# A fused recurrent attention and gated MLP kernel: another order table

## The chip, the cores and the metric

The kernel runs on one core of a Trainium2 chip. The metric is the device time of one execution in microseconds (us); the time of the kernel before is the median of three runs. A core has five engines that matter here, each with its own queue of instructions that it works through in order: TensorE (PE in the profile; PEld are its weight loads), VectorE (DVE), ScalarE (ACT), GpSimd (POOL), and SyncE (SP), which here only issues transfers. Sixteen DMA engines move the data.

## The reference

Four sequences of 768 steps go through a recurrent gated linear attention with 8 heads of width 48; its output, 4 x 768 x 384, is the input of a gated MLP that mixes over positions.

```python
for t in range(S):
    state = alpha[:, :, t, :, None] * state + np.einsum('bhd,bhe->bhde', k[:, :, t], v[:, :, t])
    y[:, :, t] = np.einsum('bhd,bhde->bhe', q[:, :, t], state)
...
h = np.maximum(x @ w_in, 0.0)                      # 384 x 1024
u, v = (h[..., :d_ff // 2].copy(), h[..., d_ff // 2:].copy())
v_n = (v - mu) / np.sqrt(var + 1e-06)
v_s = np.einsum('ts,bsd->btd', w_spatial, v_n) + b_spatial[None, :, None]
return ((u * v_s) @ w_out).astype(np.float32)      # 512 x 384
```

The inputs q, k, v and alpha are 4 x 8 x 768 x 48 in float32, and the result is float32.

## The kernel before

The recurrence is cut into 24 chunks of 128 positions, six for each sequence. Within a chunk the steps become matmuls: cumulated logarithms of alpha, scaled keys and queries, a masked score matrix, and a state that is handed on from chunk to chunk. The first eight chunks are worked in four pairs (numbered 0 to 3, function `pair`), whose loads bring two chunks at once (384 KB); the other sixteen are worked one by one (function `first`, loads of 192 KB). As soon as a sequence's chunks are done, its MLP follows in groups of matmuls (functions `second_v`, `second_u`, `second_s`, `second_o`; all through `group`, whose matmuls are recorded under line 828).

All this is made into 1,141 operations, each a few instructions for one engine. Their names are a kind and numbers, and the text uses them:

- `ac`, `kc`, `qc`, `vc` with a chunk's number (a pair's first chunk): the loads of alpha, k, q, v, all issued on SyncE's queue in the order of the table (lines 441 and 646).
- `ln`, `cum`, `einv`, `eexp`: logarithm (ScalarE), cumulated sum (TensorE, lines 461 and 666), and the exponentials of it with both signs (ScalarE, lines 469, 478, 678, 695). For a pair they are called `lnp`, `cump` and so on, with the pair's number and a half.
- `kt`, `qt` (for a pair `ktp`, `qtp`): the scaled keys (GpSimd, line 690; for a pair GpSimd or VectorE, line 483) and queries (VectorE, lines 490 and 700). `vb`, `vbp`: the values cast to bf16 (GpSimd or ScalarE).
- `trk` (line 719), for a pair `tr_k`, `tr_q` (line 511): their transposes on TensorE; `ev`: the copies of the transposes out of PSUM (VectorE or ScalarE).
- `sc` and `m`: scores (TensorE, lines 583 and 754) and their mask (VectorE, lines 594 and 765). `upd`, `z`, `S`, `sb`: the state's update (TensorE, lines 553 and 740), sum (VectorE), decay (GpSimd, line 344) and bf16 copy (`sbd`, GpSimd or VectorE, line 199).
- `ya`, `y`: the chunk's output (lines 610, 623, 776, 782). `xs`, `xt`, `xe`: its copy, its transposes (lines 374 and 398) and the copies of these.
- `v`, `bn`, `rs`, `vn`: the v half of the first MLP product, its statistics (lines 893, 894) and the normalized rows. `u`: the u half, relu'd by ScalarE or VectorE. `s` and `g`: the spatial mix (a group of six matmuls, often in two parts) and the gating product (GpSimd, line 989). `o`, `st`: the last product and its store (line 1046).
- `cast_w_in`, `cast_w_sp`, `cast_w_out`: casts of the weights out of a float32 buffer `raw_w`. Those of the spatial weights go to one of three buffers `w_row`, which `wt` (transposes on TensorE, line 840) reads; three `w_row` buffers are handed out in the order in which the casts are emitted, so the fourth cast needs the buffer that `wt` of the first has read.

Nothing reorders these operations when the kernel is built. The table `PLAN` (lines 57 to 106), found by a search beforehand, names every operation once, and `replay` emits them in that order. A word is the letter of the engine (P TensorE, D VectorE, A ScalarE, G GpSimd, S SyncE, Q a transfer's own record), the number of the operation, and for some a list of columns after colons. These are filler: before the operation takes its PSUM bank, `bank` (line 187) emits matmuls of junk with so many columns into it, whose result is overwritten. So the table sets three things: the order on each engine's queue; the engine, for the operations that may run on more than one; and the filler. It also sets indirectly who shares what, since the eight PSUM banks, the `w_row` buffers and the other tiles are given out in turn.

TensorE's array can be used whole (128 x 128) or as tiles of 64 rows (or 32, or 64 columns). The `trk`, `xt`, `wt` transposes of lines 719, 398 and 840, the pair's updates and outputs (lines 553 and 610) and the scores (lines 583 and 754) are tiled; all else is not. When a tiled and an untiled instruction follow each other, that is called a change of tiling.

Of the kernel before, what the change touches and what calls it, by code (L numbers as in the profile page):

```python
# [54 lines left out]
LETTERS = {"P": "PE", "D": "DVE", "A": "ACT", "G": "POOL", "S": "SP", "Q": "DMA"}  # L55

PLAN = """
S34 Q35 S36 Q37 G32 G0 Q33 S38 Q39 S94 Q95 S40 Q41 A42 P53:512:512:192 A54 D1 D2 D56 P43 S96 Q97 S98 Q99 S100 Q101
S163 Q164 S4 Q5 S165 Q166 S167 Q168 P59:464 G58 G48 A44 A45 A55 D46 D57 D47 P249:304 P49 P61 A50 P51 D52 D60 A62 A102
A250 P71:304 P74 P113 P103 D72 D73 D76 D75 P63 P77:172 D65 A114 D116 P119:148 A104 A64 A115 A105 A78 G66 G67 G106 D107  # L60
D117 D68 P79 P81 P111 P121 P247 P109 G3 G69 A108 A82 A80 D120 D122 D112 D110 P83 A84 A171 D248 S169 Q170 S9 Q10 S307
Q308 P131 P134 D133 D136 D132 D135 G70 G118 P172:228 P182 P123:240 A183 A8 A173 A124 P137 P138 A139 A174 G7 G6 D125
P85 G126 D128 D185 G127 G129 G175 P88 P142 P140 A86 A184 D176 D186 A143 A89 P188 P190 P180 P144 P178 A141 A191 A145
A181 P146 G11 G12 S309 Q310 S311 Q312 D130 D87 D179 D90 D189 P157 A187 A177 A158 A147 A13 P197 P200 P192 D199 D201
D198 D194 D202 P151:196 P155 A315 A193 A91 P326 P316 A327 P203 P153 P204 G195 G196 G329 A317 A328 A318 P149 A205 A154
D159 D156 D152 D330 G319 P208 P334 A209 P206 D320 P332 P324 P210 P322 D92 D335 D325 D333 D148 A207 P212 A211 A150 P347
P215 P221 A213 A160 A222 A216 S14 Q15 P223 P227 S18 Q19 D93 D323 D161 D348 D349 D214 G16 G17 A224 A228 P225 P229 A226
A21 P232 A234 D231 D230 D233 G20 P235:300 P238 S313 Q314 G331 G321 P344 P336 S367 Q368 S369 Q370 S22 Q23 S371 Q372
A237 A236 D217 D162 D346 A240 D338 A239 A218 D219 D220 A375 A337 P251 P263 P259 P376 A377 A378 G339 P264 D345 D341
D265 P260 D261 P255 P252 A380 A25 A24 D381 D253 P256 D257 G340 G342 G379 S409 Q410 S373 Q374 S446 Q447 S411 Q412 S413  # L70
Q414 S415 Q416 S26 Q27 S480 Q481 S448 Q449 S482 Q483 S450 Q451 S484 Q485 P383 A385 A417 S452 Q453 S577 Q578 S486 Q487
S581 Q582 S579 Q580 S583 Q584 P244 P241 P350 A246 D384 D245 D242 D243 P390 P354 P418 D392 D391 A351 A355 G262 G343
A420 A382 G254 G266 P279 P352 P271 P356 P393 P272 A353 A357 A419 G421 A422 A394 P280 P361 P386 P275 P395 A362 A424
A396 A31 D273 D423 D281 D387 P425 D397 D427 D426 D363 G282 G388 P276 P358 D277 P398 G258 G389 G278 G30 A399 A454 A359
A28 A488 P405 P432 P267 P455 P401 A402 A457 A456 D29 P291 P489 P268 A490 A459 D406 D433 D400 D434 D360 P283 P428 D269
D460 A492 D429 D493 G458 G491 P435 A284 A292 A436 G274 G461 G270 G430 G431 S648 Q649 S617 Q618 S650 Q651 S611 Q612
S652 Q653 S613 Q614 S690 Q691 S615 Q616 S694 Q695 S654 Q655 S692 Q693 P287 P462 P437 P495 P403 D463 D464 D497 D496
A288 A439 A438 P440 A585 A441 A364 D404 P469 P498 P295 P465 P586 P303 D471 D470 D466 D500 D499 A296 A587 A588 A590
A304 P299 G494 G467 G468 G589 G592 D591 D442 P472 A473 P501 P407 P474 A502 A300 P503 P593 P596 A443 A505 A408 D475
D476 P477 A478 D504 D366 D594 D595 D445 D444 D597 D365 P506 P600 P515 D601 D516 A507 A479 A508 D509 D602 A656 A510  # L80
A619 P517 P525 P513 P519 P529 P657 P533 P620 D511 D512 P526 P530 A514 A659 A658 A621 A661 A622 A698 A624 D518 D520
D527 D531 D662 P545 P534 P699 A701 A700 A703 D625 G598 G599 G660 G626 G623 G528 D535 P546 D547 P630 P627 P664 P537
P603 D631 D665 D704 G548 A629 A628 G632 G663 A604 P538 P634 P605 S728 Q729 S762 Q763 S696 Q697 S730 Q731 S732 Q733
S764 Q765 S766 Q767 D539 A607 A666 A606 D635 D636 P541 P667 P542 G702 G532 P706 P671 D668 D543 D673 D672 G669 G536
G670 G544 G633 P608 P637 P521 A707 A736 A708 A638 P737 P713 P639 P522 P549 D714 D715 D641 D523 A770 A609 A705 A738
A739 G740 A640 A741 D742 P771 P550 P642 A772 P709 P744 A774 A643 A746 D710 D551 D775 D745 D644 G524 S858 Q859 S734
Q735 S929 Q930 S860 Q861 G773 G711 G552 G712 G743 G540 P716 P674 A717 A675 P561 P718 P676 P777 P553 A562 A678 A677
D719 D779 D720 D610 P679 P751 A778 A554 A866 A680 A645 A681 P780 D752 P747 D748 D753 D781 D782 P682 P867 P721 P754
A868 A869 A871 A722 A755 S768 Q769 S862 Q863 A723 A776 D683 D872 P573 P688 P684 G749 G750 G870 P756 P874 D646 D757
D875 D685 D758 A689 A574 D724 A876 P686 P783 P569 P881 A784 P785 A570 A787 A687 A725 D882 D786 D883 P759 P557 A760  # L90
P788 P565 P796 P798 P800 S1042 Q1043 S971 Q972 S892 Q893 S864 Q865 S898 Q899 S896 Q897 A979 A558 A789 A566 A937 A900
S894 Q895 S935 Q936 G873 S975 Q976 S931 Q932 S933 Q934 S973 Q974 S977 Q978 S1008 Q1009 S567 Q568 S1046 Q1047 S559 Q560
S1012 Q1013 S1010 Q1011 S1044 Q1045 S1014 Q1015 D727 D647 D761 D726 P794 P806 D790 A791 D799 D797 D795 D792 D793 D801
P901 P980 P802 P938 P877 P807 A902 A903 A907 A905 A981 A939 A940 A982 A944 A984 P810 P803 A942 G904 D878 G941 G879
D808 D906 D804 G805 G880 G809 G983 D985 D943 P822 P884 P811 D812 A885 P823 P908 P886 P945 D824 P814 P911 P815 D912
D909 D816 G813 G817 G913 G825 A910 A887 A888 A947 A946 P889 A1016 A890 P952 P915 P987 D953 D916 D954 P830 P1017 P831
P818 A988 A1019 A1050 A1018 D917 P948 P819 P1051 D949 A1021 A986 A989 D1022 D832 G950 P834 A1052 G951 G1020 P990 P842
P918 A835 A1054 D820 D991 D1055 A843 A919 P838 P1024 P994 P920 D1025 D921 D995 D996 A839 A1023 G914 G833 G1053 G992
S1048 Q1049 S575 Q576 S836 Q837 S844 Q845 S293 Q294 S289 Q290 S571 Q572 S305 Q306 S301 Q302 S555 Q556 A922 A1026 S297
Q298 S285 Q286 S840 Q841 P826 P955 P827 D828 A956 P1057 P957 P1031 D958 P1027 D1028 D1033 D1032 P997 P923 A1058 A1059  # L100
A959 P969 P1060 A1056 A998 P999 D1062 D1001 D1061 D970 G821 G829 G993 G1029 A1000 A924 P960 P846 P1034 A961 A847 G1030
P1063 A1035 A1064 P1002 P963 P1036 P1065 D925 D891 A1003 D962 D1066 P850 P967 A1067 A1037 D1004 A926 D928 P1068 A964
A1038 P1039 D927 D968 A851 A1005 A1069 A1040 D1006 D1041 D1007 D1070 P965 P854 P1076 P1080 P1078 P1074 D966 A1079 A855
A1071 A1081 D1075 D1072 D1073 D1077 P1094 P1082 P1106 P1086 P1083 P1098 P1095 P1090 P1102 P1087 P1107 P1091 P1103
P1110 P1099 P1111 D1096 D1084 G1085 D1088 D1097 D1108 D1092 D1093 G1089 P1113 D1104 G1109 G1105 D1112 D1100 D1101
P1117 P1121 S852 Q853 S563 Q564 S856 Q857 S848 Q849 A1114 S1115 Q1116 A1118 P1133 S1119 Q1120 A1122 P1125 A1134 S1123
Q1124 P1129 S1135 Q1136 A1126 P1137 S1127 Q1128 A1130 A1138 S1131 Q1132 S1139 Q1140
"""


# [1046 lines left out]
```

## Time and profile before

| what | value |
|---|---|
| median of three runs | 144.78 us (144.51 to 145.1) |
| the profiled execution's own time | 144.51 us |
| its span | 142.7 us |
| granted TensorE clock | 1.00 |
| busy: PE / PEld / DVE / ACT / POOL | 134.7 / 84.8 / 118.3 / 109.3 / 83.4 us |
| DMA | 28.64 MB, mean 201 GB/s |
| longest groups on PE | spatial mix 36.8 us, `u` 18.7 us, `o` 18.7 us, `v` 17.1 us |

The span is the time from the first to the last recorded instruction; the execution's own time has some 1.8 us more around it. Busy times of an engine add up its instructions; matmuls overlap, so a busy TensorE isn't one at its peak. The chain of waits goes back from the last instruction, at each step to what released it, and so names who set the end at each moment; its rows give the start, the length and the engine and line, in us. A row of a timeline gives start and length, engine, line, operation, what it writes and reads, and in brackets how long the engine had been idle before and what ended that. A DMA share near or above 1.00 means that the 16 DMA engines had packets under way all the time.

### The profile page before, as it was taken

What the parts mean: (1) busy time and instruction counts of PE and PEld (TensorE: products, weight loads), DVE (VectorE), ACT (ScalarE), POOL (GpSimd) and SP (SyncE); (2) the same over time, 40 slices, a digit from 0 to 9 for tenths busy, and PEclk for the clock granted to TensorE, in tenths of its full rate; (3) what the DMA queues carried; (4) which work ended last, traced back from release to release, by engine and by line L of the source; (5) the groups of instructions that cost most, each with busy time, mean ns of one, the idle gap of its engine ahead of it and who ended that gap; (6) DMA issues with size and microseconds to landing.
All of it is one profiled execution on the core that took longest, in us unless ns stands there. A gap on an engine that the chain in (4) does not pass through costs nothing.

```text
span 142.7 us, 4968 instructions
## 1 busy us (share of the span) xinstructions
PE 134.7 (94%) x1912; PEld 84.8 (59%) x1923; DVE 118.3 (83%) x291; ACT 109.3 (77%) x282; POOL 83.4 (58%) x146
## 2 busy tenths in 40 slices
PE   7999798899999999999999999999999989999990
PEld 3457575566577656675666665656666656566560
DVE  7279878989989699999998898989979779994940
ACT  3477759999888969889987999997978978940061
POOL 6703977366339776982389999410799993000720
PEclk9999999999999999999999999999999999999999
DMA  4999999999998999999999998999998794113045
GB/s 106 270 261 261 321 259 256 290 289 358 236 217 160 237 226 202 194 169 203 171 196 183 182 198 140 214 152 194 191 231 165 229 341 168 56 58 111 0 161 170
DMA packets 89000, 28.64 MB, mean 201 GB/s; under 512 B 83728, under 2 KB 87440, under 8 KB 88976
## 3 DMA queue, kind: packets, MB, share of 16 engines
q1 hardware_dynamic: 88944, 28.32, 91.3%
q8 instruction: 15, 0.25, 0.8%
q14 instruction: 9, 0.07, 0.2%
q0 software_dynamic: 32, 0.00, 0.0%
HBM read 23.60 MB, written 4.72 MB: 198 GB/s over the span
## 4 chain that ended last, share of the span: by engine, by line
PE 63%; SPq 9%; POOL 7%; DMA 6%; DVE 5%; ACT 4%; issue 3%; ACTq 0%; POOLq 0%; DVEq 0%
PE bank L828 46%; SPq L441 8%; DMA qc<-in_q_dram 6%; PE bank L719 2%; PE bank L754 2%; POOL kt L690 2%; POOL gT L989 2%; POOL sbd L199 2%; PE bank L782 2%; DVE ptm L765 1%; PE bank L740 1%; PE bank L666 1%; SPq L1081 1%; PE bank L776 1%; DVE qt L490 1%
## 5 line engine op out<-in xcount | busy, mean ns | idle before, releaser
L828 PE MATMUL bank<-w_spT,vn 128*128 128x384 bf16 x192 | 36.8, 326 | 0.0
L989 POOL TENSOR_TENSOR gT<-vsb,uT 128x384 bf16<-128x384 f32 x28 | 25.7, 925 | 14.9 <-DVE vsb L976 14.4
L765 DVE TENSOR_TENSOR ptm<-bank,mask 128x512 bf16<-128x512 f32 x32 | 20.7, 682 | 1.9 <-PE bank L398 1.2
L828 PEld LDWEIGHTS <-vn 128*128 128x128 bf16 x192 | 16.6, 97 | 9.5 <-issue 0.2
L690 POOL TENSOR_TENSOR kt<-kc,binv 128x384 bf16<-128x384 f32 x16 | 14.6, 915 | 9.9 <-ACT bc L685 5.1
L976 DVE TENSOR_TENSOR vsb<-bank,bsp_bc 128x384 f32<-128x384 f32 x31 | 16.5, 551 | 4.2 <-PE bank L828 2.5
L828 PE MATMUL bank<-xT,w_in 128*128 128x384 bf16 x96 | 18.7, 326 | 0.0
L828 PE MATMUL bank<-w_out_sb,gT 128*128 128x384 bf16 (+1 forms) x100 | 18.7, 319 | 0.0
L828 PE MATMUL bank<-w_in,xT 128*128 128x512 bf16 x61 | 17.1, 379 | 0.8 <-issue 0.2
L344 POOL TENSOR_TENSOR state<-state,bc 128x192 f32<-128x192 f32 x20 | 10.4, 522 | 8.9 <-ACT bc L559 3.4
L197 ACT COPY kqT<-bank 128x512 bf16<-128x512 bf16 x21 | 12.1, 598 | 3.7 <-PE bank L719 1.1
L199 POOL CAST sbd<-state 64x192 bf16<-64x192 f32 x38 | 13.3, 350 | 2.0
L893 DVE BATCH_NORM_STATS2 stats<-v_sb 128x6 f32<-128x512 bf16 x20 | 13.6, 682 | 0.3 <-ACT v_sb L203 0.3
L203 ACT ACTIVATE v_sb<-bank 128x512 bf16<-128x512 f32 x20 | 11.7, 604 | 1.2 <-PE bank L828 1.0
L828 PEld LDWEIGHTS <-w_in 128*128 128x128 bf16 x96 | 8.8, 97 | 5.9
L828 PEld LDWEIGHTS <-gT 128*128 128x128 bf16 x100 | 8.9, 97 | 5.6 <-DVE gT L989 0.4
L199 DVE COPY kqT<-bank 128x512 bf16<-128x512 bf16 x27 | 10.4, 416 | 1.9 <-PE bank L511 1.0
L197 ACT CAST x_sb<-bank 128x384 bf16<-128x384 f32 x24 | 11.4, 489 | 0.7 <-PE bank L610 0.2
L187 PE MATMUL bank<-junk 128*128 128x512 f32 (+9 forms) x24 | 10.5, 542 | 1.1 <-DVE junk L240 1.1
L197 ACT COPY xT<-bank 128x192 bf16<-128x192 bf16 (+1 forms) x26 | 9.3, 376 | 1.7 <-PE bank L398 1.1
L594 DVE TENSOR_TENSOR ptm<-bank,mask 128x512 bf16<-128x512 f32 x16 | 10.2, 682 | 0.5 <-PE bank L583 0.3
L197 ACT COPY o_sb<-bank 128x384 f32<-128x384 f32 x9 | 4.4, 484 | 8.0 <-PE bank L828 8.0
(126 smaller groups left out, 285.4 us busy)
## 6 DMA issues: line engine op xcount, KB each, us to landing
ac<-in_alpha_dram SPq DMA_DIRECT2D x16, 192.0 KB, 4.4
kc<-in_k_dram SPq DMA_DIRECT2D x16, 192.0 KB, 4.9
qc<-in_q_dram SPq DMA_DIRECT2D x16, 192.0 KB, 4.3
vc<-in_v_dram SPq DMA_DIRECT2D x16, 192.0 KB, 4.4
raw_w<-in_moe_w_spatial_dram SPq DMA_DIRECT2D x3, 768.0 KB, 6.7
out_dram<-raw_w SPq DMA_DIRECT2D x11, 192.0 KB, 2.7
out_dram<-o_sb SPq DMA_DIRECT2D x9, 192.0 KB, 1.9
ac<-in_alpha_dram SPq DMA_DIRECT2D x4, 384.0 KB, 6.2
```

Of the source, the lines that this page charges most:

```text
L187: nc.tensor.matmul(out=flat[:, 0:cols].rearrange("p (a b) -> p a b", a=4), lhsT=junk, rhs=junk[:, None, 0:n].to_broadcast([128, 4, n]), st ...
L197: nc.scalar.copy(out=out, in_=in_)
L199: ENG[eng].tensor_copy(out=out, in_=in_)
L203: nc.scalar.activation(out=out, in_=in_, func=AF.Relu)
L344: ENG[eng].tensor_tensor(out=st["state"], in0=st["state"], in1=st["bc"][:, :, None].to_broadcast([128, HP, D]), op=ALU.mult)
L441: nc.sync.dma_start(out=t.rearrange("p h a d -> p h (a d)"), in_=src[b, :, t0:t0 + 2 * C, :].rearrange("h (p a) d -> p h (a d)", a=2))
L690: ENG[eng].tensor_mul(out=k_blocks(kt3)[:, :, :, 0:D], in0=quad(st["kc"]), in1=st["binv"])
L765: nc.vector.tensor_tensor(out=st["ptm"][:, s], in0=st[f"pt{s}"], in1=mask4, op=ALU.mult)
L828: return lambda ps: nc.tensor.matmul(out=out(ps), lhsT=lhsT(), rhs=rhs(), start=start, stop=stop)
L893: nc.vector.bn_stats(out=stats, in_=d["v_sb"][:, tt, :])
L976: nc.vector.tensor_tensor(out=hold["vs"], in0=ps[:, 0:TH], in1=bsp_bc[:, th, :], op=ALU.add)
L989: ENG[eng].tensor_tensor(out=bt[b]["gT"][:, dsl, cols], in0=hold["vs"], in1=bt[b]["uT"][:, dsl, cols], op=ALU.mult)
```

## The change

The whole table `PLAN` is replaced by another that the search found when it moved further away from where it began and put a higher price on TensorE's changes of tiling. Everything else stays: the operations, their instructions, buffers and types. The new table differs in the order of all five queues almost from the first line on, in the engine of some operations, and in the filler (13 words with 3,848 columns instead of 12 with 3,572).

By operations, VectorE gives eight `u` copies, eight `ev` copies and one bias copy to ScalarE and takes three casts of `w_in`, eight `xe` copies and one `sb`; GpSimd takes six casts of values and one of the spatial weights, and gives two casts of `w_in` and one `sb` away; ScalarE gives up what the other two took.

The diff replaces 49 lines by as many; shown are the first 14 of each (up to the first spatial mix) and those around chunks 22 and 23. To find one's way: S307 is the load `ac` of pair 3, S163, S165, S167, S169 are `ac`, `kc`, `qc`, `vc` of pair 2, S4 and S9 the two halves of `w_in`; G11 to G13 (or A13, D11) cast the second half; G195, G196 are `S` and `sb` of chunk 4, P204 and P208 `y` of chunks 4 and 5; G20 and A21 or G21 are the casts of spatial tiles 2 and 3, P229, P232, P235, P238 the transposes `wt` 0 to 3; G1020 and G1053 are `kt` of chunks 22 and 23, G833 a gating product, P1024 `trk` of chunk 22.

```diff
-S34 Q35 S36 Q37 G32 G0 Q33 S38 Q39 S94 Q95 S40 Q41 A42 P53:512:512:192 A54 D1 D2 D56 P43 S96 Q97 S98 Q99 S100 Q101
-S163 Q164 S4 Q5 S165 Q166 S167 Q168 P59:464 G58 G48 A44 A45 A55 D46 D57 D47 P249:304 P49 P61 A50 P51 D52 D60 A62 A102
-A250 P71:304 P74 P113 P103 D72 D73 D76 D75 P63 P77:172 D65 A114 D116 P119:148 A104 A64 A115 A105 A78 G66 G67 G106 D107
-D117 D68 P79 P81 P111 P121 P247 P109 G3 G69 A108 A82 A80 D120 D122 D112 D110 P83 A84 A171 D248 S169 Q170 S9 Q10 S307
-Q308 P131 P134 D133 D136 D132 D135 G70 G118 P172:228 P182 P123:240 A183 A8 A173 A124 P137 P138 A139 A174 G7 G6 D125
-P85 G126 D128 D185 G127 G129 G175 P88 P142 P140 A86 A184 D176 D186 A143 A89 P188 P190 P180 P144 P178 A141 A191 A145
-A181 P146 G11 G12 S309 Q310 S311 Q312 D130 D87 D179 D90 D189 P157 A187 A177 A158 A147 A13 P197 P200 P192 D199 D201
-D198 D194 D202 P151:196 P155 A315 A193 A91 P326 P316 A327 P203 P153 P204 G195 G196 G329 A317 A328 A318 P149 A205 A154
-D159 D156 D152 D330 G319 P208 P334 A209 P206 D320 P332 P324 P210 P322 D92 D335 D325 D333 D148 A207 P212 A211 A150 P347
-P215 P221 A213 A160 A222 A216 S14 Q15 P223 P227 S18 Q19 D93 D323 D161 D348 D349 D214 G16 G17 A224 A228 P225 P229 A226
-A21 P232 A234 D231 D230 D233 G20 P235:300 P238 S313 Q314 G331 G321 P344 P336 S367 Q368 S369 Q370 S22 Q23 S371 Q372
-A237 A236 D217 D162 D346 A240 D338 A239 A218 D219 D220 A375 A337 P251 P263 P259 P376 A377 A378 G339 P264 D345 D341
-D265 P260 D261 P255 P252 A380 A25 A24 D381 D253 P256 D257 G340 G342 G379 S409 Q410 S373 Q374 S446 Q447 S411 Q412 S413
-Q414 S415 Q416 S26 Q27 S480 Q481 S448 Q449 S482 Q483 S450 Q451 S484 Q485 P383 A385 A417 S452 Q453 S577 Q578 S486 Q487
...
-P818 A988 A1019 A1050 A1018 D917 P948 P819 P1051 D949 A1021 A986 A989 D1022 D832 G950 P834 A1052 G951 G1020 P990 P842
-P918 A835 A1054 D820 D991 D1055 A843 A919 P838 P1024 P994 P920 D1025 D921 D995 D996 A839 A1023 G914 G833 G1053 G992
-S1048 Q1049 S575 Q576 S836 Q837 S844 Q845 S293 Q294 S289 Q290 S571 Q572 S305 Q306 S301 Q302 S555 Q556 A922 A1026 S297
...
+S34 Q35 S36 Q37 G32 G0 Q33 S38 Q39 S94 Q95 S40 Q41 A42 P53:512:512:192 A54 D1 D2 D56 P43 S96 Q97 S98 Q99 S163 Q164
+S100 Q101 S4 Q5 S167 Q168 S165 Q166 P59:464 G58 G48 A55 A44 A45 D46 P49:292 D57 D47 P61 P51 P249 A50 A62 D60 D52
+P74:232 P71 D76 D75 D72 A102 A250 P113 P103 A114 A115 D116 A104 P63:264 G106 P119:148 P247 P109 A64 A105 A110 A248
+A120 D65 D73 D107 D117 P111:276 P121 A171 D112 G66 D122 D68 P134:304 P131 P77 D67 D133 D136 D135 D132 S307 Q308 S169
+Q170 S9 Q10 A118 A78 P172 A173 A108 P79 P81 P182 A82 P83 P123 P137 A183 A80 A84 A7 A124 A174 G3 G69 G70 D8 D6 D125
+P138 A139 A184 G126 G127 P85 P88 A89 D176 D186 D128 D175 D90 P140 P142 P180 A143 P178:256 P190 P144 A141 A86 A145 G129
+G185 P188:168 G130 G177 G187 A191 D181 D179 P157 A189 A315 A158 D87 P197 P146 S311 Q312 S309 Q310 S14 Q15 P200 P326
+P316 D198 D199 D201 D202 P192 P203 G13 G12 D194 D11 P204 A327 A147 A317 A193 A91 A328 A205 A318 P149 P151 G195 G196
+P206 P208 P153 G329 G319 D148 D330 D92 D320 A209 A207 A150 P334 P210 P324 A211 A325 P212 P332 A154 A213 D152 D93 D159
+D333 D335 P225 D226 A160 D214 D161 P215 P347 P221 P322 A216 A323 P227 A228 A222 D348 D349 P223 G16 G17 P229 P232 S18
+Q19 G20 P235:228 D217 D233 D234 D236 A224 A230 A231 D237 P344 P155 S313 Q314 S367 Q368 S369 Q370 S22 Q23 S371 Q372
+G321 G331 P336 S373 Q374 S480 Q481 S409 Q410 S411 Q412 S413 Q414 A375 A218 P376 A377 A337 A378 A156 D162 D345 P251
+D219 D220 D338 D346 A380 G21 P259 S26 Q27 G379 G339 P252 D253 P260 D261 D341 G342 G340 P238 P263 P255 P264 D381 D265
+P256 D257 G382 G262 G343 G258 G254 G266 A25 A240 A24 A239 S415 Q416 S484 Q485 S446 Q447 S482 Q483 S448 Q449 S450 Q451
...
+A1016 A890 S977 Q978 S1012 Q1013 S571 Q572 S1042 Q1043 A989 D988 D916 P948 D949 D953 P830 P1017 P831 D954 D917 D832
+P842 A986 A1018 A1019 A1050 A1021 A843 P834 P838 A835 A839 G825 G914 G950 P990 P1051 A1052 A1054 D1022 D991 D891 S1010
+Q1011 G951 G1020 S1044 Q1045 S1014 Q1015 D1055 S285 Q286 S293 Q294 S1048 Q1049 S559 Q560 S575 Q576 S301 Q302 S297 Q298
+S305 Q306 S844 Q845 S840 Q841 S836 Q837 S555 Q556 S289 Q290 P818 P918 P819 D820 A919 A1023 G1053 G992 G833 G821 P1024
...
```

## The prediction

> **What bounds the kernel now.** I read the summary first, then the slices, a table by stretches, the chain of waits, and the timelines of TensorE, GpSimd and SyncE around each break of the chain.
>
> ```profile
> PE 134.7 (94%) x1912; PEld 84.8 (59%) x1923; DVE 118.3 (83%) x291; ACT 109.3 (77%) x282; POOL 83.4 (58%) x146
> PE 63%; SPq 9%; POOL 7%; DMA 6%; DVE 5%; ACT 4%; issue 3%; ACTq 0%; POOLq 0%; DVEq 0%
> ```
>
> TensorE is busy for 94% of the span and holds 63% of the chain; no other engine holds a tenth, but all hold something. The stretches say where (columns: length, then busy time of TensorE, its weight loads, VectorE, ScalarE, GpSimd, then granted clock, DMA share, GB/s):
>
> ```profile
> 0.00:27.40 27.40, 24.20 (x358) 14.88 (x360) 20.48 (x59) 18.67 (x39) 15.30 (x38) 1.00 1.07 253
> 27.40:40.00 12.60, 12.33 (x225) 8.21 (x224) 12.05 (x31) 11.24 (x29) 7.27 (x12) 1.00 1.08 295
> 40.00:78.00 38.00, 37.77 (x591) 24.17 (x592) 34.58 (x86) 32.47 (x90) 26.91 (x44) 1.00 1.06 195
> 78.00:115.00 37.00, 36.15 (x543) 23.17 (x541) 32.53 (x77) 33.77 (x92) 26.16 (x43) 1.00 1.04 192
> ```
>
> TensorE is nearly full from 27 us on, the clock is 1.00 throughout, and the DMA engines are full (1.04 to 1.08) until 115 us: the loads come as a steady stream, and the order of the table decides which of them is late. The chain between 22 and 41 us is where TensorE is not yet its own bound:
>
> ```profile
> 13.96 8.82 DMA qc<-in_q_dram
> 27.01 0.42 PE bank L583 x16
> 28.22 0.53 PE bank L187 x2
> 31.79 0.55 DVE qt L490
> 37.48 0.30 PE bank L840 x12
> 37.90 0.84 POOL w_row L199
> 38.78 0.53 PE bank L840 x24
> ```
>
> The q load of pair 2 (pairs count from 0) holds the chain until 22.8 us, then VectorE's queue until 27.0; two filler matmuls (line 187) stand before the first `u` group, which waits for the second half of `w_in`; at 31.79 VectorE's `qt` makes TensorE wait; at 37.90 a GpSimd cast into `w_row` does, and that cast itself waited for TensorE's transposes (line 840) to free the buffer. Later the chain is TensorE's own, but for one long break:
>
> ```profile
> 111.31 0.92 POOL kt L690
> 113.09 0.91 POOL gT L989
> 114.01 0.88 POOL kt L690
> 114.93 0.41 PE bank L719 x16
> ```
>
> GpSimd puts a gating product between the `kt` of chunks 22 and 23, and TensorE waits for the second.
>
> I measure progress as lag: clock time minus the TensorE work already done. Work is a count of matmuls by their spacing: twelve of 384 columns took 1.95 us in the chain (100.78), so 162.5 ns each; 512 columns take 216 ns; the small ones 23 to 56 ns. All real matmuls are 114.0 us, the 75 changes of tiling 7.8, so 121.75; the last one ends at 139.05, a lag of 17.3, and 3.65 of copy and store follow (142.70). Lag is 14.3 at the first `u` group (28.6), 15.3 at the first spatial group (40.4), 16.0 at 78, 17.1 at 115, 17.4 at 137. Only lag and tiling changes can move: the work is the same. The profiled run took 144.51, 1.81 around its span, and is the lowest of three; the median, 144.78, is 0.27 above it.
>
> **The change, part by part.** Only the table differs. Counted by instruction, consecutive matmuls change their tiling 72 times instead of 75.
>
> ```profile
> 57.74 0.65 PE bank L828 x4
> 58.39 0.34 PE bank L719 x16
> 58.73 0.12 PE bank L398 x6
> 58.86 0.23 PE bank L719 x16
> ```
>
> Sixteen transposes of line 719 take 0.34 us after a 128-row matmul and 0.23 after a 64-row one: 0.11 per change (0.095 into, 0.118 out of 64 rows as means). Three fewer: **-0.31** (bounds -0.2 and -0.5). The Trainium skill, TensorEngine Tiling (Array Packing), Key Properties, says that a change of mode drains TensorE, without a price; with the fixed part of a pass from TensorE: Matmul & The Clock Gate, Single matmul latency (398 cycles at 2.4 GHz, 0.166 us) as an estimate of a drain, three would be 0.50; the rows say 0.31, and I go by them.
>
> *Work moved between engines.* By mean durations, VectorE loses 3.2 us (115.1 to 111.9: eight `u` copies and eight `ev` go to ScalarE, against three `w_in` casts and eight `xe`), ScalarE gains 1.9, GpSimd 1.8 (six value casts `vb`/`vbp` and a spatial cast more, two `w_in` casts fewer). By the stretches VectorE has 2 to 4 us to spare in 37, ScalarE 3 to 6, GpSimd 10: nothing directly.
>
> *Head, to the first `u`.* On SyncE's queue pair 2's q load now precedes its k load, so q lands one pair load (1.5 us, the usual distance of their landings) earlier, and the chain's break at 22.8 is taken by k, whose factor is one VectorE product instead of two; VectorE also loses the two `sbd` casts (0.68) standing there. That gains about 1 us. Pair 3's alpha load (1.5) now precedes pair 2's v load and the second half of `w_in`, both 1.5 later. In the timeline of GpSimd:
>
> ```profile
> 27.21 1.17 POOL L199 CAST w_in<-raw_w 128x512 bf16<-128x512 f32 x2 [2.99 <-DMA raw_w<-in_moe_w_in_dram]
> ```
>
> The cast waited for the landing (27.15). Now: 28.65 + 1.17, first `u` at 29.9; but 1.37 us more TensorE work stands before it (two `cump` .65, one `ya` .55, one `y` .17), so the lag is 14.25 against 14.28: **0**. The 1 us gained is the cover of this landing; if it is gone, the landing costs nothing more, since `u` starts at 29.9 either way; a still later landing costs all it is late.
>
> *To the first spatial group.* Before, ScalarE's cast of spatial tile 3 was emitted ahead of GpSimd's cast of tile 2, so tile 2's had to reuse the buffer that transpose `wt_0` held; now tile 2's comes first. That takes away the 0.84 at 38.78 (inside it ran 0.7 us of filler, which goes too) and, with pair 3's transposes reordered, the 0.25 at 32.38. Added: `y_5` waits 0.2 for GpSimd's `sb_4`, queued behind the `w_in` casts (as are `S_4` and, behind it, pair 3's `kt`), and filler of 228 columns before `wt_2`, some 0.45. 1.09 removed, 0.65 added: **-0.4** (bounds -1.1, all removed and nothing added, and +0.2, the waits replaced and filler on top).
>
> *From there to the end.* Before, lag grows by 2.16: named waits are 0.18 at 64, 0.21 at 83.4, 0.16 at 87.9, 0.40 at 114.9, 0.25 after 133, 0.08 at 92.9, together 1.28; 0.88 is in gaps too small to name. After, `kt_23` directly follows `kt_22`, 0.9 earlier: that takes the 0.40, and what stands behind it starts earlier. The other waits may go or be put elsewhere: the table shows similarly small reserves, 0 to 0.5 us, in bank reuse around chunks 13 and 14. The floor is the stream: with landings in the new order (1.07 us per load of 192 KB) and the chain behind each, chunks 10 to 17 need a lag of 14.8 to 15.2. I take 1.66 growth instead of 2.16: **-0.5**, nearest to the one wait whose cause is removed (bounds -1.6, on the stream's floor plus the tail's 0.25 and 0.3 of small gaps, and +1.0, half as much waiting again in a table whose waits nobody has seen).
>
> Sum: -0.31 + 0 - 0.4 - 0.5 = -1.2: the profiled run 143.3, the median 143.6.
>
> **The rivals.**
> *The waits are only moved.* GpSimd carries two more `vb` casts (0.48 each, 0.96) between `kt_16` and `kt_23`, with each `kt` and its transposes queued behind; they eat the 0.9 gained at `kt_23`, and the 0.5 is lost, as is the 0.4 if `y_5` and filler cost what the removed waits did. Then -0.3: 144.5. For it: GpSimd held the chain for 4 us before 114.9. Against: it idles 10 us of that stretch.
>
> *The stream decides, and the kernel is slower.* Forecast lag is 15.4 to 15.6 where chunk 17 needs 15.22, so 0.4 is all the cover that 64 loads have left. If they land 0.04 apart more (1.11 instead of 1.07; single distances lie between 0.7 and 1.8), the last are 2.6 us late, 2.2 beyond the cover: 145.8. It decides from 0.4 us of slip on. For it: a DMA share over 1.04 through 115 us, and a third store now issued ahead of the last value load. Against: same bytes, same packets, one queue.
>
> *The head decides.* `w_in` is needed at 28.65; each microsecond later goes to the end in full. Landings of its two halves took 3.07 and 3.47: 0.4 alone gives 144.0; two pair loads' worth (3.0), half of it covered by work that can be run first, gives 145.1, and with `y_5`'s chain behind it 145.6.
>
> *On the floor.* All bounds taken together but the worst of tiling: -0.3 - 0.6 - 1.3 = -2.2: 142.6.
>
> *It doesn't do what it says.* Three changes of 75 is all that a higher price on them bought; alone that is 0.2%, beneath what can be told (0.5%, 0.72 us). This is the first rival's time.
>
> **How the numbers follow.** Forecast .43 (142.9 to 144.1, its own range), floor .07, moved waits .22, stream .16, head .08, something unseen and slower .04. Faster by 0.5% means below 144.06, slower above 145.50. Faster: .43 + .07 = .50; same: .22; slower: .16 + .08 + .04 = .28. The time is the forecast's, 143.6; the range goes from the floor to the stream's rival, 142.5 to 145.8.
>
> **What the profile after would show.** Twelve-matmul groups unchanged in spacing; the first `u` at 29.9 with the `w_in` cast just before; no wait for `w_row` at `wt_2`; `kt_22` and `kt_23` back to back and no wait of 0.4 at the transposes after; lag near 14.9 at the first spatial group, 15.5 at work 62 us (78 on the clock), 16.5 at the end. Wrong if TensorE's waits name loads (`kc`, `ac`, `vc`) between 40 and 110 us, if the first `u` is later than 30.5, or if lag grows by over 2.2 after the spatial group. A span under 142 would say that VectorE's lightening, which I priced at nothing, was worth it.

## The result and the profile after

The changed kernel takes 146.61 us in the median of six executions (145.76 to 147.18), the one before 144.70 in its six: a ratio of 1.0112 (95% interval 1.0073 to 1.0152). The change makes the kernel slower by 1.1%, where I had forecast 0.8% faster. The profiled execution took 147.18, with a span of 145.4 and a mean granted clock of 0.988. Of the six, two were at 0.988 (147.16 and 147.18) and four at 1.000 (145.76 to 146.65), so there are two things to explain: some 1.6 us in every execution, and 0.85 us more in some.

The summary of the page, the granted clock in 40 slices, and the shares of the chain:

```profile
PE 137.7 (95%) x1925; PEld 85.2 (59%) x1925; DVE 117.9 (81%) x287; ACT 110.8 (76%) x283; POOL 85.4 (59%) x149
PEclk9999986999999999999999999999999999999999
PE 68%; DVE 12%; SPq 6%; DMA 5%; ACT 3%; issue 2%; ACTq 0%; DVEq 0%
```

TensorE still holds the chain, but VectorE has gone from 5% to 12% of it, and GpSimd from 7% to nothing. One slice of the clock reads 6. The chain shows four breaks (start, length, what). The first, in the head:

```profile
10.22 7.61 DMA vc<-in_v_dram
17.85 0.03 ACT vbp L197
18.27 0.48 ACT x_sb L197
18.80 0.34 PE bank L374 x3
```

TensorE's transposes of chunk 0 (line 374) wait for ScalarE's copy `x_sb`, which stands in ScalarE's queue behind the cast of pair 1's values, which waits for their load. In the timeline of ScalarE, the cast's row has the wait in brackets:

```profile
15.80 0.87 ACT L452 ACTIVATE la<-ac 128x768 bf16<-128x768 f32 x1
17.85 0.51 ACT L197 CAST vbp<-vc 128x384 bf16<-128x384 f32 x1 [1.19 <-DMA vc<-in_v_dram]
18.27 0.47 ACT L197 CAST x_sb<-bank 128x384 bf16<-128x384 f32 x1
```

The table by stretches of 2 us (length, then busy time of TensorE, its weight loads, VectorE, ScalarE, GpSimd, then the clock, DMA share, GB/s) shows what follows:

```profile
18.00:20.00 2.00, 0.87 (x10) 0.49 (x11) 1.58 (x4) 2.00 (x6) 0.00 (x0) 1.00 1.24 278
20.00:22.00 2.00, 2.00 (x80) 1.92 (x81) 1.06 (x3) 2.00 (x6) 0.21 (x1) 0.72 1.06 249
22.00:24.00 2.00, 2.00 (x7) 0.62 (x5) 1.55 (x4) 0.89 (x3) 1.01 (x4) 0.50 0.84 201
24.00:26.00 2.00, 2.00 (x26) 1.65 (x25) 1.07 (x3) 1.45 (x4) 1.89 (x4) 0.93 0.85 293
```

TensorE is busy for 0.87 of 2 us, and 2 to 3 us later its clock is halved, for 3.4 us: seven matmuls take two microseconds. The second break is where I had credited the table with a removed wait:

```profile
37.80 1.21 DVE ptm L594 x2
39.05 0.33 PE bank L840 x11
39.38 0.58 PE bank L187 x2
39.97 0.28 PE bank L840 x12
```

No cast into `w_row` appears any more; VectorE's masks hold the second half of the transposes `wt_1`, and filler (line 187) follows. In this execution the chain lies mostly on VectorE from 28.1 to 39.0 us (in the run a0_after, used below, from 34.4 to 38.0). The third break:

```profile
107.97 0.67 DVE sbd L199
108.64 0.09 issue
108.73 0.21 DVE sbd L199
108.94 0.59 issue
109.53 0.42 DVE kqT L199
110.00 0.32 PE bank L666
```

VectorE makes the state copy `sb` of chunk 18, the copy `kqT` of chunk 21 stands behind it, and TensorE's cumulated sum of chunk 22 waits for the bank that this frees. The `kt` of chunks 22 and 23 that held the chain before are not on it. The fourth is the end:

```profile
135.01 1.66 DVE gT L989 x2
136.80 1.50 DVE vsb L976 x3
138.32 1.32 DVE gT L989
139.69 0.42 PE bank L828 x3
140.16 1.57 PE bank L828 x9
```

VectorE's gating products set when the last matmuls can start.

Since the profiled execution is one with the slow clock, lags are read below from a second profile of the same kernel, at a clock of 0.995 (run a0_after, span 144.4). Lag is counted as in the prediction:

| place | before | forecast | after, a0_after |
|---|---|---|---|
| first `u` group | 14.28 | 14.25 | 14.59 |
| first spatial group | 15.3 | 14.9 | 16.1 |
| at 78 us | 16.0 | 15.5 | 16.9 |
| first `o` after the sum of chunk 22 | 16.6 | | 18.2 |
| last products | 17.4 | 16.5 | 19.45 |

The end is 2.02 later in lag; less 0.31 for three tiling changes, that is the 1.7 by which the spans differ (144.4 and 142.7).

### The profile page after: what moved, and what is told of

It reads as the page before. It is cut to its first block, busy times and chain, and to the rows that moved or that the text cites. A ratio compares the mean times of both kernels' runs of the same rounds, so it can differ in the third digit from the quotient of the medians.

```text
span 145.4 us, 4968 instructions
## 1 busy us (share of the span) xinstructions
PE 137.7 (95%) x1925; PEld 85.2 (59%) x1925; DVE 117.9 (81%) x287; ACT 110.8 (76%) x283; POOL 85.4 (59%) x149
## 4 chain that ended last, share of the span: by engine, by line
PE 68%; DVE 12%; SPq 6%; DMA 5%; ACT 3%; issue 2%; ACTq 0%; DVEq 0%
PE bank L828 48%; SPq L441 6%; DMA vc<-in_v_dram 5%; PE bank L719 3%; PE bank L754 3%; DVE ptm L594 3%; DVE vsb L976 2%; PE bank L782 2%; PE bank L666 2%; DVE gT L989 2%; PE bank L740 2%; PE bank L776 2%; PE bank L398 1%; DVE vn L925 1%; PE bank L840 1%
## 5 line engine op out<-in xcount | busy, mean ns | idle before, releaser
L828 PE MATMUL bank<-w_in,xT 128*128 128x512 bf16 x72 | 20.0, 399 | 0.1
L828 PE MATMUL bank<-xT,w_in 128*128 128x384 bf16 x96 | 19.4, 326 | 0.0
L197 ACT COPY kqT<-bank 128x512 bf16<-128x512 bf16 x29 | 16.3, 600 | 4.1 <-PE bank L511 2.4
L828 PE MATMUL bank<-w_out_sb,gT 128*128 128x384 bf16 (+1 forms) x100 | 18.6, 320 | 0.5 <-DVE gT L989 0.4
L199 POOL CAST sbd<-state 64x192 bf16<-64x192 f32 x36 | 12.4, 344 | 1.9
L187 PE MATMUL bank<-junk 128*128 128x512 f32 (+11 forms) x26 | 11.4, 540 | 1.1 <-DVE junk L240 1.1
L203 ACT ACTIVATE uT<-bank 128x384 bf16<-128x384 f32 x22 | 10.6, 502 | 1.2 <-PE bank L828 1.1
L925 DVE TENSOR_SCALAR vn<-v_sb,mvs,rstd 128x512 bf16<-128x512 bf16 x24 | 10.0, 440 | 1.0 <-ACT rstd L918 0.9
L828 PEld LDWEIGHTS <-xT 128*128 128x128 bf16 x72 | 6.7, 102 | 6.6 <-issue 1.1
```

The costliest lines, as they stand in the source:

```text
L187: nc.tensor.matmul(out=flat[:, 0:cols].rearrange("p (a b) -> p a b", a=4), lhsT=junk, rhs=junk[:, None, 0:n].to_broadcast([128, 4, n]), st ...
L197: nc.scalar.copy(out=out, in_=in_)
L199: ENG[eng].tensor_copy(out=out, in_=in_)
L203: nc.scalar.activation(out=out, in_=in_, func=AF.Relu)
L828: return lambda ps: nc.tensor.matmul(out=out(ps), lhsT=lhsT(), rhs=rhs(), start=start, stop=stop)
L925: nc.vector.tensor_scalar(out=d["vn"][:, t, :], in0=d["v_sb"][:, t, :], scalar1=d["mvs"][:, t, 0:1], scalar2=d["rstd"][:, t:t + 1], op0=AL ...
```

## The experiments

They ran on several chips, on each beside the kernel before, whose median there was 144.3 to 145.3; so ratios to before are compared. Where before had 145.3 (v2, s1, w1 and f1) the new table was not run without a change. f1 ends there with a0_after's lag (19.5), but its ratio is 1.0059 against a0_after's 1.0109, so these ratios can't be set against those of other chips: what v2, s1 and w1 gain is read from their traces and isn't shown by the times. In the diffs a word of the table is written with its operation's name in place of its number, D(x) for x on VectorE, and so on; words of other engines that stand between the words shown are left out.

**Head and rest exchanged.**

```diff
 # h1_head_before: words of before up to the first spatial group, then what is left in after's order
 # h2_head_after: words of after up to the first spatial group, then what is left in before's order
```

> The order of before up to the first spatial group, and from there on the order of after. Lag (clock time less TensorE work done) at the first spatial group was 15.27 in before's trace and 16.96 in after's, and afterwards it grew by 2.16 and 3.48. Theory A, the head costs 1.2 to 1.7 us of its own and the later stretches the rest: lag at the first spatial group 15.2 to 15.4, growth after it about 3.4, time 145.0 to 145.4. Rival B, the later waits of after were only the late head's echo (an engine that ran behind since then): growth 1.7 to 2.2, time 143.5 to 144.2. Rival C, an earlier head only waits longer later, for loads: lag at 78 us as in after, time 146.3 or more.

> The order of after up to the first spatial group, and from there on the order of before. Theory A: before plus the head's loss, 145.9 to 146.4, a wait of about 1 us of TensorE near 18 us for a copy x_sb behind a load of v. Rival B, what is lost in the head is made up later, where TensorE waits anyway (0.18 at 64, 0.21 at 83, 0.16 at 88, 0.40 at 115 in before): 144.9 to 145.4.

Ratios 1.020 (1.014 to 1.026) and 1.019 (1.014 to 1.025): each mixture is slower than both kernels. Theory A had 145.0 to 145.4 and 145.9 to 146.4; Rival C of the first had such a time, by waits for loads further on, which is not where the loss lies. Where the two orders join, operations that one table had already emitted and the other not come in an order that nobody planned: in h1 the lag jumps from 15.43 at `wt_2` to 16.69 at the sum of chunk 8, in h2 from 17.05 to 20.52 within the first spatial groups. In h1 TensorE waits for ScalarE's logarithm, behind a cast into `w_row` and five copies of `w_spT`; in h2 the transposes `wt_3` wait 1.81 for ScalarE's cast. So the times say nothing of the head. What can be read is the growth after the seam, from the scores of chunk 8 to the end: 3.4 in h1 and 3.3 in a0_after (after's order), 2.0 in h2 and 2.0 in before (before's order). The later part of the new table costs 1.4 however late its head is; it is no echo.

**The tail.**

```diff
 # t1_tail_before: words of after up to the first spatial group of sequence 3, then before's order
```

> The order of after up to the first spatial group of the last sequence, and from there on the order of before. In after the lag grew by 0.75 from 136.7 us to the last product, where VectorE's gating products took 1.2 and 1.31 us beside GpSimd's, against 0.56 alone; in before by 0.15, with one of 1.09. Theory A, the tail's order costs 0.5 to 0.8 of its own: 145.8 to 146.1, one slow gating product on VectorE, last lag 0.6 lower. Rival, the tail waits because what precedes it is late: no change, 146.4 to 146.8.

Ratio 1.0069 (1.0038 to 1.0099). From the sum of chunk 22 to the end the lag grows by 0.5 instead of 1.25. That is Theory A: the tail's order has a cost of its own.

**What makes VectorE's products long.**

```diff
-G(g_3_1_1) G(g_3_2_1) D(g_3_0_1)
+D(g_3_1_1) D(g_3_2_1) D(g_3_0_1)
```

> After, with the last two gating products of GpSimd on VectorE, which then has three in a row and GpSimd none. In after VectorE's product beside them took 1.31 us, and 0.56 where GpSimd was idle. Theory A, the two engines' products hinder each other: each of the three takes 0.5 to 0.6, so VectorE ends within 0.3 us of where it ended with one, and the time stays within 0.4 us of after's. Rival, VectorE's product is long for another reason (its input comes late): one of them still takes over 1 us, and the tail gets 0.7 to 1.1 longer.

Ratio 1.012, as after. VectorE's timeline after the tail's third `vsb`, first of after, then of g1:

```profile
136.80 1.49 DVE L976 TENSOR_TENSOR vsb<-bank,bsp_bc 128x384 f32<-128x384 f32 x3
138.32 1.31 DVE L989 TENSOR_TENSOR gT<-vsb,uT 128x384 bf16<-128x384 f32 x1
```

```profile
136.78 1.49 DVE L976 TENSOR_TENSOR vsb<-bank,bsp_bc 128x384 f32<-128x384 f32 x3
138.18 1.49 DVE L989 TENSOR_TENSOR gT<-vsb,uT 128x384 bf16<-128x384 f32 x3
139.58 0.55 DVE L969 TENSOR_TENSOR gT<-bank,uT 128x384 bf16<-128x384 f32 x1
```

Three products take 1.49 when GpSimd is idle; one takes 1.31 when GpSimd multiplies beside it. The `vsb` sums before it, which read one operand from PSUM, take 0.5 each in both. So two engines working at the same time finished no sooner than one alone. The Trainium skill, SBUF — State Buffer, section "SBUF: two separate sides", states a rule for this: a VectorE instruction in a mode that uses two ports, or with two SBUF inputs beside a GpSimd instruction that reads SBUF, shares a pair of ports with GpSimd; whichever starts first has the pair for its whole instruction, and the other waits. The trace agrees for the two-input products (1.27 and 1.31 beside GpSimd, 0.55 alone) and for the `vsb` sums, which are not longer beside it. The rule would have given a warning before any run; a price needs to know which instructions run at the same moment.

**The state copy of chunk 18.**

```diff
-D(sb_18)
+G(sb_18)
```

> After, with only the state copy sb of chunk 18 on GpSimd instead of VectorE. In after its two casts took 1.64 us on VectorE from 107.97 while GpSimd ran three gating products (the same two take 0.72 on GpSimd, and 0.68 on VectorE in before at 23.9), and TensorE waited 0.6 for the copy kqT queued behind them, lag up by 0.7 at the cumulated sum of chunk 22. Theory A, those two casts set that wait: lag there 0.4 to 0.7 lower, time 145.8 to 146.2. Rival B, GpSimd's queue gets 0.7 longer and its kt of chunk 21 and the gating products come later: wait of the same size within the next 5 us, time 146.2 to 146.9.

Ratio 1.0048 (1.0016 to 1.0079). VectorE and GpSimd in after:

```profile
107.97 1.64 DVE L199 CAST sbd<-state 64x192 bf16<-64x192 f32 x2
```

```profile
107.69 2.69 POOL L989 TENSOR_TENSOR gT<-vsb,uT 128x384 bf16<-128x384 f32 x3
```

and GpSimd in s1:

```profile
104.94 0.72 POOL L199 CAST sbd<-state 64x192 bf16<-64x192 f32 x2
```

The same two casts take 1.64 on VectorE beside three products of GpSimd and 0.72 on GpSimd. The wait at the sum of chunk 22 is gone. About 0.3 comes back in waits at the transposes of chunks 21 and 22, for GpSimd's `kt` behind the copy (Rival B, in part). The last lag is 18.64, 0.8 under a0_after's, of which about 0.2 was there before the change's place is reached.

**The hole at 18 us and the clock.** The hole is the wait of 1.16 at the transposes of chunk 0 (in a0_after 1.00). Three attempts on it: the load in its old place, ScalarE's queue in another order, filler in the hole.

```diff
 # v1_vc2_first
-S(ac_4) S(vc_2)
+S(vc_2) S(ac_4)
 # v2_act_order
-A(vbp_1_1) A(xs_0) A(einvp_2_0) A(vbp_1_0) A(xs_1)
+A(xs_0) A(einvp_2_0) A(xs_1) A(vbp_1_1) A(vbp_1_0)
 # f1_filler
-P(cump_2_0)
+P(cump_2_0):300
```

> After, with only pair 1's v load issued ahead of pair 2's alpha load again, as in before. In after ScalarE's queue stood at a cast of these values until they landed at 17.8 us, with the copy x_sb of chunk 0 behind it, and TensorE waited 1.16 us; then the granted clock fell to 0.5 for 3 us. Theory A, that load made the wait and the wait the slow clock: the landing comes at about 16.4, no wait over 0.4 near 18 us, clock 1.00 in every run, time 145.3 to 145.8. Rival B, the wait goes to the next load (pair 2's alpha, 1.5 us later, then its logarithm and exponentials): 146.3 to 146.7, with a TensorE wait for binvp or qt between 20 and 25 us. Rival C, the slow clock has another cause: it is still seen in about one run of three.

> After, with ScalarE's two casts of pair 1's values moved behind its two copies x_sb of chunks 0 and 1 (the loads stay as in after). Theory A, the wait of 1.2 us at 18 us is not the load's own but the place of a load-bound instruction ahead of a ready one in ScalarE's queue: the copy of chunk 0 starts at about 17.3 instead of 18.2 and no wait over 0.3 is left before the transposes of chunk 0. What it is worth then depends on what comes next, since pair 1's update needs the casts at 17.8 and about 1 us after: lag at the first u group 0.3 to 0.8 lower than in an undisturbed run of after (14.47), the clock at 1.00 in nearly all runs, time 145.3 to 145.9 against some 146.4 of after. Rival B, the chain behind the third pair's keys and queries sets the first u group anyway: TensorE waits a little later, at the update or at the third pair's transposes, time 146.2 to 146.7, and the slow clock is seen less often or not at all only if the hole before it is filled.

> After, with 300 columns of filler (0.8 us) ahead of the first cumulated sum of pair 2, which lies in the hole of TensorE between 17.4 and 18.8 us. Theory A, that hole, followed by the one of 0.3 at 19.6, is what lowers the granted clock to 0.5 from 21.4 to 24.4 us in some of the executions (two of six in after, two of twelve with before's tail): no execution with a clock under 0.995, median 0.2 to 0.5 under after's, 146.0 to 146.4, and the best executions no better than after's best, 145.8. Rival, the clock drops for another reason: it still does in one of three to six executions.

v1: 1.0179 (1.0135 to 1.0223), worse than after: the logarithm of pair 2, which also stands ahead of `x_sb` in ScalarE's queue, now waits for its load instead, and a hole of 1.19 is left.

```profile
10.21 7.26 DMA ac<-in_alpha_dram
17.48 0.02 issue
17.50 0.03 ACT la L452
17.53 0.72 issue
18.25 0.49 ACT vbp L197
18.75 0.39 ACT x_sb L197
19.13 0.05 issue
19.18 0.34 PE bank L374 x3
```

Rival B. v2: 1.0068 (1.0034 to 1.0102); the transposes of chunk 0 start at 17.79 instead of 18.6 to 18.8. The gain at the first `u` group is 0.25 (14.34), a little less than Theory A had, for the second half of `w_in` is next: it landed at 29.0, and the chain goes through it, as it does in c1 below.

```profile
21.14 7.86 DMA raw_w<-in_moe_w_in_dram
29.05 0.81 POOL w_in L199 x2
```

f1: 1.0059 (1.0030 to 1.0088), with the lags of a0_after up to the scores of chunk 16 within 0.35. The filler shortened the hole; it didn't close it: 0.85 is left before the transposes of chunk 0.

On the clock the three differ clearly. Executions whose mean clock was under 0.99: after 2 of 6, a0_after 2 of 8, t1, s1 and w1 2 of 12 each, g1 1 of 4, v1 5 of 6, together 16 of 60; their profiles have a hole of 0.97 to 1.52 there. With the queue reordered, which leaves gaps of at most 0.3 there (v2, and c1 to c4 below): none of 61. With the hole shortened to 0.85 (f1): none of 12, too few to say much. The mixtures add h1 with 4 of 6 and h2 with 2 of 6; h1 has before's head without the hole at 18 us, but a gap of 1.26 at its seam, and in h2's profile the clock falls twice, once after the head's hole and once after a gap of 1.81 at its seam. So gaps of about a microsecond let the clock fall in some executions. They don't always: the profiles of a0_after, t1, s1 and w1 have the hole and a clock of 0.995 or more, and v2's has a gap of 1.2 at 79.7 us, from its late load, and a clock of 1.00. And they aren't its only cause: before itself has 8 of 106, and no gap over 0.42 in its profile; what happened in those 8 stays open. The Trainium skill, TensorE: Matmul & The Clock Gate, section "HAM oscillation — how this bites in real kernels", asks for no idle gap over about 3.4 us. Here the longest gap was 1.16 us, with one of 0.34 behind it, and the clock fell; the measurement decides.

**The filler and the buffer at `wt_2`.**

```diff
 # w1_no_filler, in after
-P(wt_2):228
+P(wt_2)
 # b1_two_fixes, in before
-A(cast_w_sp_1_1) ... G(cast_w_sp_1_0) P(wt_2):300
+G(cast_w_sp_1_0) A(cast_w_sp_1_1) ... P(wt_2)
-G(g_2_3_1) G(kt_23)
+G(kt_23) G(g_2_3_1)
```

> After, without the filler of 228 columns ahead of the transposes wt of spatial tile 2. In after 0.26 of a wait for VectorE's mask and then 0.58 of filler stand there. Theory A, the filler is on the path: lag behind it 0.4 to 0.6 lower, time 145.8 to 146.1. Rival B, it only fills a wait (for the bank that VectorE's and ScalarE's copies of the tiles before still hold): a wait of 0.3 to 0.6 takes its place, 146.3 to 146.6.

> Before with two things alone that the forecast credited to the new table: GpSimd's cast of spatial tile 2 emitted ahead of ScalarE's of tile 3 (so that it doesn't reuse the buffer that wt_0 holds), with the 300 columns of filler ahead of wt_2 gone, and GpSimd's gating product moved from between the kt of chunks 22 and 23 to behind them. As the forecast priced them (0.84 and 0.40) and if nothing takes their place: lag at wt_2 14.5 to 14.7 instead of 15.3, no wait at the transposes of chunk 23, time 0.9 to 1.2 below before, ratio 0.992 to 0.994. Rival, VectorE is full there (its masks and statistics run without a gap from 28 to 39 us), so that a wait for its mask or its copies of w_spT takes the first one's place, and the second one is all: 0.2 to 0.5 below before, ratio 0.9965 to 0.9985. Rival, both are taken by what comes next: within 0.1.

w1: 1.0100 (1.0059 to 1.0141), no gain that can be told. In its trace the lag at `wt_2` is 0.4 under a0_after's, as Theory A had it. Behind that its profiled execution had two late loads, of spatial tiles at 37 us and of `w_out` at 53.03, which by itself held TensorE for 1.5 us; such single late loads were seen in v2 (alpha of chunk 16, at 80.28) and c4 too. b1: 1.0011 (0.9977 to 1.0044), where the forecast's prices gave 0.992 to 0.994. Both waits are gone from the places where the forecast removed them: lag at the transposes of chunk 23 no longer jumps, and three `wt` run through:

```profile
36.96 0.89 PE L840 MATMUL bank<-ident,w_row 64*128 64x64 bf16 x36
38.50 0.35 PE L840 MATMUL bank<-ident,w_row 64*128 64x64 bf16 x12 [0.65 <-ACT w_row L197]
```

But the first wait has only moved: ScalarE's cast of tile 3 is now the fourth, the one that needs the buffer that `wt_0` reads, and `wt_3` waits 0.65 for it. Of the 0.84 some 0.2 is gained. In the profiled execution loads took the rest: `w_out` landed at 52.58 (52.3 in before), where the gain ends, and the last load of alpha at 106.86, against 104.57 in before. Its logarithm stands in ScalarE's queue ahead of a copy that frees a bank for the sum of chunk 22, which waits:

```profile
100.97 5.89 DMA ac<-in_alpha_dram
106.88 0.52 ACT la L660
107.41 0.50 ACT v_sb L203
107.94 0.32 PE bank L666
```

That costs as much as the moved product gains at chunk 23 (0.40), and the end is where it was (lag 17.63, before 17.43). The forecast had credited these two changes with 1.24; in before the twelve times show nothing of it. By the times the rival "both are taken by what comes next" is right, but what took the second one in the other executions isn't shown, and VectorE, which the first rival named, isn't what took the first. In the new table tile 3's cast and `wt_3` stand 4 us later, so what happens there is read from c2 and c3.

**The unaltered table again, and three parts taken back.**

```diff
 # c1_three, in after
-A(vbp_1_1) A(xs_0) A(einvp_2_0) A(vbp_1_0) A(xs_1)
+A(xs_0) A(einvp_2_0) A(xs_1) A(vbp_1_1) A(vbp_1_0)
-D(sb_18)
+G(sb_18)
 # and from the first spatial group of sequence 3 on, before's order
```

> The changed kernel unaltered, on the same chip as the three beside it, as their measure. Executions at a clock of 0.995 or more some 1.1% over before's, about one in five at 0.984 to 0.988 and 0.9 us slower still; in an undisturbed profile lag 14.5 at the first u group, 15.8 at the first spatial group, 17.9 at the cumulated sum of chunk 22 and 19.3 at the end.

> After with three parts taken back together: ScalarE's two casts of pair 1's values behind its two copies x_sb, the state copy of chunk 18 on GpSimd, and the last sequence from its spatial groups on in before's order. Theory A, the three costs lie one behind the other and add: 0.3 + 0.5 + 0.65 less than the unaltered table at full clock, and no slow clock: ratio to before 0.998 to 1.004, final lag 17.7 to 18.1 (before 17.4, with 0.31 more tiling changes in its work). Rival B, the stream of loads, 1 to 2 us behind before's from the middle on, is what remains: TensorE waits for loads (ac, kc or w_out) take back most of it, ratio 1.004 to 1.008.

a0_after: 1.0109 (1.0072 to 1.0146), as the first measurement. c1: 0.9993 (0.9959 to 1.0026), final lag 17.48, no execution with a slow clock. Both ran on the same chip. With the three parts taken back, the whole loss is gone, and nothing is left over for the load stream: in the profiles of before, a0_after and c1 the 61st of the 87 loads to land does so at 83.1, 83.4 and 82.7 us.

**What holds `wt_2`.** All three start from c1.

```diff
 # c2: both changes; c3: the first alone; c4: the second alone
-D(bn_0_4) D(vn_0_2) D(m_3_1_0) D(m_3_1_1)
+D(m_3_1_0) D(m_3_1_1) D(bn_0_4) D(vn_0_2)
-P(wt_2):228
+P(wt_2)
```

> The version with three parts taken back (lag 14.66 at tr_k_3_1, 15.51 at wt_2, 17.48 at the end; ratio to before 0.9993), with VectorE's two masks of pair 3's second half ahead of the statistics and the normalisation that stood before them, and without the 228 columns of filler ahead of wt_2. Theory A, mask and filler are all that holds wt_1 and wt_2: lag at wt_2 14.6 to 14.9, and if nothing later eats it, final lag 0.5 to 0.8 lower, ratio 0.994 to 0.997. Rival B, the copies of w_spT that free the next banks, or the first spatial group's normalised rows, wait instead: lag at the first spatial group 15.2 to 15.6, ratio 0.998 to 1.001.

> The same with the masks first and the filler kept. Theory A: the wait of 0.2 to 0.3 in the middle of wt_1 goes, the filler's 0.58 stays, lag at wt_2 15.1 to 15.3, ratio 0.997 to 0.999. Rival B: the filler hides the wait anyway, lag at wt_2 15.4 to 15.6, ratio as without it, 0.999.

> The same with the masks where they were and without the filler. Theory A: lag at wt_2 0.5 to 0.6 lower, 14.9 to 15.0, ratio 0.995 to 0.998. Rival B, the filler filled a wait: lag at wt_2 or at the operation after it 15.2 to 15.5, ratio 0.998 to 1.000.

c3: 0.9992 (0.9958 to 1.0025); the wait in `wt_1` is gone, lag at `wt_2` 15.24 instead of 15.51, and 17.24 at the end (Theory A in the trace, too small for the time to tell). c2: 1.0036 (1.0007 to 1.0064); lag at `wt_2` is 14.79, and 15.50 again 4 us later, at a spatial group that waits for VectorE's normalised rows:

```profile
39.79 0.60 DVE ptm L594
40.39 1.25 DVE vn L925 x2
41.64 0.05 issue
41.69 0.34 PE bank L828
```

Rival B: VectorE is the limit from 34 to 42 us, and what TensorE gains at the transposes it loses to the rows. c4: 0.9971 (0.9949 to 0.9993), 0.2 us under before in the median (144.09 and 144.31; c3 has 143.98). Its profiled execution had late loads again, so that the trace doesn't show why it does better than c2. It is the only version whose interval lies under 1; that is one of fifteen comparisons, and c3's median is lower still, so that either beats before isn't shown.

## Why the prediction was wrong, step by step

- **Tiling, -0.31.** The change is there (72 changes), and in after's chain the sixteen transposes take 0.34 after a 128-row matmul and 0.23 after a 64-row one, as before. With equal lag at the end (c1 17.48, before 17.43) the spans are 142.5 and 142.7. The price stands, if only to the 0.2 that these two show.
- **"Nothing directly" for moved work.** This failed first. I compared sums of mean durations and each engine's idle time. But in these traces VectorE's durations depend on what GpSimd does at that moment: two casts 1.64 instead of 0.7, products 1.27 and 1.31 instead of 0.56. The row that could have warned me was in before's trace: one gating product of 1.09 beside GpSimd's, against 0.56.
- **Head to the first `u`, 0.** What I followed was right in the main: in the runs with the new order of loads the second half of `w_in` landed at 27.9 to 29.3 (forecast 28.65), and at the full clock the first `u` started at 29.6 to 30.3 (29.9). What I left out was another exchange on SyncE's queue, pair 1's v load behind pair 2's alpha load. It landed at 17.8 instead of 15.1, and the new table had a cast of it ahead of a ready copy in ScalarE's queue. In place of the 1 us gained that I took as cover stood a hole of 1.0 to 1.2: lag +0.3 at the first `u`, or +1.5 with the slow clock. (In a0_after's own profile `w_in` landed at 29.26 and is on the chain too; in t1, s1 and f1, where it landed at 27.9 to 28.4, `u` started hardly earlier, at 30.1 to 30.3.) I took the clock as 1.00 because it was so in before.
- **To the first spatial group, -0.4.** About +0.5 (from 1.0 before to 1.5 in a0_after between the first `u` and there). The wait for `w_row` went as predicted, the filler cost the 0.58 that I had put at 0.45, and the term that failed is the 0.25 to 0.84 removed: VectorE's queue is the next limit, 0.26 at `wt_1` at once (c3), more within 4 us when both are removed (c2). In before, too, the removed wait mostly moved, there to ScalarE's cast (b1).
- **To the end, -0.5.** +1.2. The 0.40 at chunk 23 went as predicted; alone, in b1, nothing of it shows in the time. I had listed VectorE's takeover of one `sb` without looking where it stood (0.6 to 0.7, s1), and gave what the new tail might add no term at all (0.7 to 0.8, t1). The upper bound of +1.0 was too small by little; I gave it no weight.
- **The rivals.** The slower case I gave 16% was the load stream. It is real in single executions (in w1 one late load held TensorE for 1.5 us) but not what separates the kernels: b1 has such a load with before's order, and c1 has after's order of loads up to the last sequence and before's time. The right answer, several costs of 0.5 to 0.8 in different places, lay a little beyond the sum's upper bounds (+0.3, +0.5 and +1.2 against 0, +0.2 and +1.0) and in no rival.

## What to carry to other kernels

Before crediting a removed wait, name the engine that is next in line at that place and how much room it has: here it was ScalarE's cast in the one table and VectorE's masks and rows in the other, and 1.24 us of waits removed in before showed nothing in the time. When instructions move between VectorE and GpSimd, look at what the other one does at the moment they run, not at sums. In a queue that works in order, an instruction that waits for a load must not stand ahead of one that is ready, and a hole of a microsecond on TensorE may cost a second one by the clock.

## What the runs showed that I had not expected

The granted clock fell to 0.50 for 3.4 us after holes of 1.16 and 0.34 us. Executions with a mean clock under 0.99 were 16 of 60 with such a hole at 18 us, and none of 61 where it was closed; where filler shortened it to 0.85, none of 12. Half of one good table and half of another were worse than either, by 0.8 to 2%: the seam alone cost 1.3 and 3.5 us of lag.
